# A decode step with grouped attention on one core: K transposed by VectorE as 4-byte words, V as the stationary operand, and a new order of the loads

## The chip, the cores and the metric

The kernel runs on one core of a Trainium2 chip. The time is device microseconds, from the first to the last work of one execution. Repeated executions agree within 1.5% for the kernel before. The profile is one execution, and its span is some 1.3 to 1.9 us shorter than the time. Medians are over all runs of a kernel, and slow ones are named where they matter.

Words used below. PE is the matrix engine, PEld its loading of stationary operands ("weights"), DVE is VectorE, ACT is ScalarE, SP is the engine whose queue issues the loads. A matmul contracts over the partitions (128 in the large ones here): it takes a stationary operand (here at most 128 columns) and a moving operand (some columns that stream through).

## The reference, cut to what matters

```python
# x: 1 x 512.  k_cache, v_cache: 8 heads x 16384 keys x 128, bf16.  32 query heads, 4 per K/V head.
q = layernorm(x) @ wq                      # wq 512 x 4096
scores = q . k * 128**-0.5                 # per head 4 x 16384
o = softmax(scores) @ v
h = x + o @ wo                             # wo 4096 x 512
y = layernorm(h)
# [cut] one token: the shifted groups of the mixer are all zeros, so w1 and w2 drop out
h2 = h + y + gelu(layernorm(y) @ w3) @ w4  # w3 512 x 1792, w4 1792 x 512
```

79.17 MB have to be read: 33.6 MB of K, 33.6 MB of V, 4.2 MB each of wq and wo, 3.7 MB of w3 and w4. The arithmetic is small.

One caution. With these inputs the scores are tiny and attention is nearly a plain mean, so the comparison with the reference on the chip cannot see a wrong order of keys.

## The kernel before

K arrives with keys on the partitions. For the scores it is needed with the 128 dimensions on the partitions, so PE transposes 128x128 blocks into PSUM, DVE copies eight of them at a time to SBUF, and PE uses the copies as stationary operands. In the value matmuls the probabilities are stationary (4 columns) and V moves (128 columns).

```python
# PE: transposes and scores of one block of 4096 keys
t = eng.transpose(T_ps[bb][:, u, :], knv[:, j, :], ident[:, :])
...                                                      # [cut: waits; the scores trail by one group of 8]
eng.matmul(s_ps[B % 2][:, j*REP:(j+1)*REP], kts[pb][:, u, :], QT_sb[:, REP*g:REP*g+REP])
# DVE
eng.tensor_copy(kts[bt % 2][:, :, :], T_ps[bt % 2][:, :, :])
# PE: values
eng.matmul(og[g % 2][0:REP, 0:128], ptile[:, j, :], vb[i][:, j, :], ...)
# SP: the loads, block by block (4 blocks of 1 MB per head, 8 buffers for K, 8 for V)
issue_K(B); issue_V(B)          # in the last head: all K, then all V
wq_piece(g + 1); wo_piece(g)    # 512 KB each, in rows of 1 KB
if B == 16: w3 ...              # the MLP weights in the middle of the stream
if B == 20: w4 ...
# closing of a head (FINALIZE): denominators, division, a small transpose, 16 matmuls with wo
```

The softmax here doesn't subtract the row's maximum and nothing guards it: scores larger than these inputs give would overflow.

Of the kernel before, what the change touches and what calls it, by code (L numbers as in the profile page):

```python
# [12 lines left out]
D = 512  # L13
HQ = 32
HKV = 8
SK = 16384
DH = 128
REP = HQ // HKV
# [4 lines left out]
TB = 4096  # L23
NJ = TB // 128
NBG = SK // TB
NBT = HKV * NBG
NKV = 8
OGW = 136
SCALE = 1.0 / math.sqrt(DH)
EPS = 1e-5  # L30
GELU_C = 0.044715
GELU_S = math.sqrt(2.0 / math.pi)

KMODE = ['p'] * NBT
NBATCH = 8
assert NJ % NBATCH == 0


def bass_sequential_preLN__gqa_block_cached__mixer_s_mlp__decode_kernel(
# [14 lines left out]
    with ctx:  # L54
        sb = lambda name, shape, dt: ctx.enter_context(nc.sbuf_tensor(name, shape, dt))
        ps = lambda name, shape, dt: ctx.enter_context(nc.psum_tensor(name, shape, dt))
        semaphore = lambda name: ctx.enter_context(nc.semaphore(name))

        xrow = sb("xrow", [128, D], BF16)
        row_sb = sb("row_sb", [128, D], BF16)  # L60
        ones_b = sb("ones_b", [128, 8], BF16)
        xs_f = sb("xs_f", [128, NCH], FP32)
        ln1 = sb("ln1", [128, 2 * NCH], FP32)
        ln2 = sb("ln2", [128, 2 * NCH], FP32)
        ln3 = sb("ln3", [128, 2 * NCH], FP32)
        st = sb("st", [128, 16], FP32)
        sti = sb("sti", [128, 4], mybir.dt.int32)
        c15 = sb("c15", [128, 1], FP32)
        xn_bf = sb("xn_bf", [128, NCH], BF16)
        xc_bf = sb("xc_bf", [128, NCH], BF16)  # L70
        attn = sb("attn", [128, 2 * NCH], FP32)
        xsum = sb("xsum", [128, NCH], FP32)
        final_bf = sb("final_bf", [128, NCH], BF16)
        ones_f = sb("ones_f", [128, 128], FP32)
        ident = sb("ident", [128, 128], BF16)
        act_scr = sb("act_scr", [128, 2], FP32)
        QT_sb = sb("QT_sb", [128, HQ], BF16)
        OT_sb = sb("OT_sb", [128, HQ], BF16)
        og_sb = [sb(f"og_sb{i}", [128, DH], BF16) for i in range(2)]
        rden = sb("rden", [128, 2], FP32)  # L80
        p_sb = [sb(f"p_sb{i}", [128, 4 * NJ], BF16) for i in range(2)]
        accden = [sb(f"accden{i}", [128, 16], FP32) for i in range(2)]
        rsb = [sb(f"rsb{i}", [128, REP], FP32) for i in range(2)]
        kts = [sb(f"kts{i}", [128, NBATCH, 128], BF16) for i in range(2)]
        gtmp = sb("gtmp", [128, 3 * NHC], FP32)
        hf = sb("hf", [128, NHC], FP32)
        hcol = sb("hcol", [128, NHC], BF16)
        wq_sb = sb("wq_sb", [128, NCH, 2 * REP * DH], BF16)
        wo_sb = sb("wo_sb", [128, 2 * REP, D], BF16)
        w3_sb = sb("w3_sb", [128, NCH, FM], BF16)  # L90
        w4_sb = sb("w4_sb", [128, NHC, D], BF16)
        kb = [sb(f"kb{i}", [128, TB], BF16) for i in range(NKV)]
        vb = [sb(f"vb{i}", [128, NJ, 128], BF16) for i in range(NKV)]

        s_ps = [ps(f"s_ps{i}", [128, 4 * NJ], FP32) for i in range(2)]
        og = [ps(f"og{i}", [128, OGW], FP32) for i in range(2)]
        misc_ps = ps("misc_ps", [128, 96], BF16)
        OT_ps = misc_ps[:, 0:8]
        ln_ps = misc_ps[:, 16:32].bitcast(FP32)
        e_ps = misc_ps[:, 32:96].bitcast(FP32)  # L100
        T_ps = [ps(f"T_ps{i}", [128, NBATCH, 128], BF16) for i in range(2)]
        row_ps = ps("row_ps", [128, D], FP32)

        sem_x = semaphore("sem_x")
        sem_xps = semaphore("sem_xps")
        sem_rowps = semaphore("sem_rowps")
        sem_rowsb = semaphore("sem_rowsb")
        sem_wq = [semaphore(f"sem_wq{i}") for i in range(HKV)]
        sem_wo = [semaphore(f"sem_wo{i}") for i in range(HKV)]
        sem_w34 = semaphore("sem_w34")  # L110
        sem_out = semaphore("sem_out")
        sem_kt = [semaphore(f"sem_kt{i}") for i in range(NKV)]
        sem_vb = [semaphore(f"sem_vb{i}") for i in range(NKV)]
        sem_pool = semaphore("sem_pool")
        sem_identz = semaphore("sem_identz")
        sem_onesf = semaphore("sem_onesf")
        sem_qps = semaphore("sem_qps")
        sem_s = semaphore("sem_s")
        sem_v = semaphore("sem_v")
        sem_t = semaphore("sem_t")  # L120
        sem_den = semaphore("sem_den")
        sem_otps = semaphore("sem_otps")
        sem_attnps = semaphore("sem_attnps")
        sem_lnmm = semaphore("sem_lnmm")
        sem_hid = semaphore("sem_hid")
        sem_o2 = semaphore("sem_o2")
        sem_dve = semaphore("sem_dve")
        sem_c = semaphore("sem_c")
        sem_lnin = semaphore("sem_lnin")
        sem_xn = semaphore("sem_xn")  # L130
        sem_qT = semaphore("sem_qT")
        sem_rsum = semaphore("sem_rsum")
        sem_ognorm = semaphore("sem_ognorm")
        sem_otsb = semaphore("sem_otsb")
        sem_attnc = semaphore("sem_attnc")
        sem_xc = semaphore("sem_xc")
        sem_glu = semaphore("sem_glu")
        sem_hcol = semaphore("sem_hcol")
        sem_final = semaphore("sem_final")
        sem_p = semaphore("sem_p")  # L140
        sem_gexp = semaphore("sem_gexp")
        sem_ve = semaphore("sem_ve")
        sem_rstd = semaphore("sem_rstd")
        sem_acta = semaphore("sem_acta")
# [3 lines left out]
        wq_in = A_wq.rearrange("(k p) c -> p k c", p=128)  # L148
        wo_in = A_wo.rearrange("(h d) c -> d h c", d=128)
        w3_in = B_w3.rearrange("(k p) c -> p k c", p=128)  # L150
        w4_in = B_w4.rearrange("(m d) c -> d m c", d=128)

        def k_block_rows(B):
            g, blk = divmod(B, NBG)
            return A_k_cache[0, g, blk * TB:(blk + 1) * TB, :]

        def v_block_in(B):
            g, blk = divmod(B, NBG)
            return A_v_cache[0, g, blk * TB:(blk + 1) * TB, :].rearrange("(p j) d -> p j d", p=128)

        @block.sync
        def _(eng):
            def wq_piece(g):
                if g >= 2:
                    eng.wait_ge(sem_qps, g - 1)
                slot = g % 2
                eng.dma_start(wq_sb[:, :, slot * 512:(slot + 1) * 512], wq_in[:, :, g * 512:(g + 1) * 512]
                              ).then_inc(sem_wq[g], 16)

            def wo_piece(g):  # L170
                if g >= 2:
                    eng.wait_ge(sem_attnps, g - 1)
                slot = g % 2
                eng.dma_start(wo_sb[:, REP * slot:REP * (slot + 1), :],
                              wo_in[:, REP * g:REP * (g + 1), :]).then_inc(sem_wo[g], 16)

            eng.dma_start(xrow[0:1, :], A_x[0, 0:1, :]).then_inc(sem_x, 16)

            def issue_K(B):
                i = B % NKV  # L180
                if B >= NKV:
                    eng.wait_ge(sem_s, B - NKV + 1)
                if KMODE[B] == 'x':
                    eng.dma_start(kb[i][:, :], k_block_rows(B), transpose=True).then_inc(sem_kt[i], 16)
                else:
                    eng.dma_start(kb[i][:, :].rearrange("p (j d) -> p j d", d=128),
                                  k_block_rows(B).rearrange("(p j) d -> p j d", p=128)
                                  ).then_inc(sem_kt[i], 16)

            def issue_V(B):  # L190
                i = B % NKV
                if B >= NKV:
                    eng.wait_ge(sem_v, B - NKV + 1)
                eng.dma_start(vb[i][:, :, :], v_block_in(B)).then_inc(sem_vb[i], 16)

            LAST_G0 = NBT - NBG
            for B in range(NBT):
                i = B % NKV
                g, blk = divmod(B, NBG)
                if B < LAST_G0:  # L200
                    issue_K(B)
                    if B == 0:
                        eng.dma_start(wq_sb[:, :, 0:512], wq_in[:, :, 0:512]).then_inc(sem_wq[0], 16)
                    issue_V(B)
                elif B == LAST_G0:
                    for BB in range(LAST_G0, NBT):
                        issue_K(BB)
                    for BB in range(LAST_G0, NBT):
                        issue_V(BB)
                if blk == 1 and g + 1 < HKV:  # L210
                    wq_piece(g + 1)
                if blk == 2:
                    wo_piece(g)
                if B == 16:
                    eng.dma_start(w3_sb[:, :, :], w3_in).then_inc(sem_w34, 16)
                if B == 20:
                    eng.dma_start(w4_sb[:, :, :], w4_in).then_inc(sem_w34, 16)
            eng.wait_ge(sem_rowsb, 1)
            eng.dma_start(out[0, 0:1, :], row_sb[0:1, :]).then_inc(sem_out, 16)
            eng.wait_ge(sem_out, 16)  # L220
# [16 lines left out]
        def _(eng):  # L237
# [10 lines left out]
            def qT_group(g):  # L248
                if g == 0:
                    eng.wait_ge(sem_xn, 1)  # L250
# [407 lines left out]
```

## Time and profile before

| | before |
|---|---|
| time, median of the runs beside the changed kernel | 229.29 us |
| profiled span | 228.9 us |
| last load of weights, K or V complete | 201.3 us |
| from there to the end | 27.6 us |
| PE busy / DVE busy | 82% / 45% |

The page's table in 40 slices of 5.7 us. The digits are busy tenths; PEclk is the granted clock of PE in tenths; DMA is the mean busy share of the 16 DMA engines, and GB/s is what they moved.

```profile
PE   1696999799979997999879962799997999798733
PEclk9997999999967999799999997559997999769955
DMA  5999999999999999999999999999999999600000
GB/s 202 419 408 393 422 417 401 395 419 411 398 403 409 422 395 411 406 418 410 401 403 411 392 383 395 403 412 421 403 400 406 421 417 409 261 15 3 0 3 0
```

DMA stands at 9 (90% or more) through slice 34 at about 400 GB/s: the stream never pauses. After it come one slice at 6 and five in which DMA is nearly idle and PE works on, part of the time at half clock (granted 0.52 from 200 to 205 us, 0.50 from 220 us on). Shares of busy time hide this. PE's 82% looks like the bound, yet up to 195 us PE never holds up the loads: the DMA share is 1.00 or more in every stretch of 5 us from 10 to 195 us.

The costliest groups (line, engine, operation, tiles and shapes, count | busy us, mean ns of one | idle time before, and what ended it):

```profile
L538 DVE COPY kts<-T_ps 128x1024 bf16<-128x1024 bf16 x128 | 86.2, 692 | 95.5 <-PE T_ps L295 95.5
L295 PE MATMUL T_ps<-ident,kb 128*128 128x128 bf16 x1024 | 87.1, 235 | 9.3 <-issue 9.1
L325 PE MATMUL og<-vb,p_sb 128*4 128x128 bf16 x1024 | 67.9, 230 | 0.1
```

These are the transposes, their copies and the value matmuls: the work that the change removes or reshapes.

The end in stretches of 5 us (busy time and count by engine, then granted clock, DMA share, GB/s):

```profile
core 0: us, PE busy (x) PEld busy (x) DVE busy (x) ACT busy (x) POOL busy (x), PEclk, DMA share, GB/s
190.00:195.00 5.00, 4.73 (x96) 4.24 (x94) 2.50 (x5) 0.82 (x8) 0.00 (x0) 1.00 1.01 412
195.00:200.00 5.00, 3.56 (x70) 3.12 (x68) 2.69 (x9) 0.00 (x0) 0.00 (x0) 0.79 0.65 250
200.00:205.00 5.00, 5.00 (x80) 5.00 (x78) 3.21 (x5) 0.82 (x8) 0.00 (x0) 0.52 0.09 28
205.00:210.00 5.00, 4.25 (x89) 3.97 (x86) 2.03 (x3) 0.35 (x4) 0.00 (x0) 1.00 0.01 3
```

The tail in order of time (start, duration, engine, line, operation):

```profile
207.37 0.35 PE L266 MATMUL s_ps<-QT_sb,kts 128*128 128x4 bf16 x8 [0.61 <-DVE kts L538]
207.66 7.31 PE L325 MATMUL og<-vb,p_sb 128*4 128x128 bf16 x128
...
227.40 0.26 SPq L219 DMA_DIRECT2D out_dram<-row_sb  x1
```

The last scores of head 7 end at 207.7 us, 6.4 us after the last load. Then 128 value matmuls take 7.3 us (57 ns each), then come wo, the layer norm, the MLP and the output, one after the other, to 228.9 us. Almost nothing of this overlaps with a load.

### The profile page before, as it was taken

How to read it: one execution, taken by the hardware profiler on the slowest of the kernel's cores; microseconds unless marked ns; L12 is line 12 of the kernel's file. 1: busy time of each engine (PE TensorE's matmuls, PEld its weight loads, DVE VectorE, ACT ScalarE, POOL GpSimd, SP SyncE). 2: the span in 40 equal slices, each digit the busy share in tenths (PEclk: the TensorE clock that was granted, in tenths of full speed). 3: DMA queues.
4: the chain of work that ended last, by engine and by line, in shares of the span. 5: the costliest groups of instructions: out<-in, count | busy, mean ns of one | idle time of the engine just before them, and what ended most of it. 6: DMA issues, size and time to landing. Idle time of an engine off the chain costs nothing.

```text
span 228.9 us, 7736 instructions
## 1 busy us (share of the span) xinstructions
PE 186.8 (82%) x3477; PEld 169.7 (74%) x3477; DVE 103.4 (45%) x226; ACT 28.3 (12%) x260; POOL 0.7 (0%) x7
## 2 busy tenths in 40 slices
PE   1696999799979997999879962799997999798733
PEld 1585888688869885988768852698887888698633
DVE  4371555355534445245435530525551445561263
ACT  2011111012101111111101200111110112101000
POOL 1000000000000000000000000000000000000000
PEclk9997999999967999799999997559997999769955
DMA  5999999999999999999999999999999999600000
GB/s 202 419 408 393 422 417 401 395 419 411 398 403 409 422 395 411 406 418 410 401 403 411 392 383 395 403 412 421 403 400 406 421 417 409 261 15 3 0 3 0
DMA packets 20036, 79.66 MB, mean 348 GB/s; under 512 B 1314, under 2 KB 11300, under 8 KB 11812
## 3 DMA queue, kind: packets, MB, share of 16 engines
q1 hardware_dynamic: 20004, 79.17, 87.0%
q8 instruction: 27, 0.44, 0.8%
q14 instruction: 5, 0.04, 0.0%
HBM read 79.17 MB, written 0.00 MB: 346 GB/s over the span
## 4 chain that ended last, share of the span: by engine, by line
PE 65%; DVE 22%; issue 9%; DMA 3%; SPq 0%; ACT 0%; DVEq 0%
PE og L325 29%; PE T_ps L295 21%; DVE kts L538 17%; PE s_ps L266 9%; DMA wq_sb<-in_A_wq_dram 3%; PE misc_ps L346 2%; PE misc_ps L259 1%; DVE og_sb L554 1%; PE misc_ps L336 1%; PE og L332 1%; DVE OT_sb L560 1%; DVE rden L552 1%; DVE rsb L546 1%; PE misc_ps L386 0%; DVE row_sb L627 0%
## 5 line engine op out<-in xcount | busy, mean ns | idle before, releaser
L538 DVE COPY kts<-T_ps 128x1024 bf16<-128x1024 bf16 x128 | 86.2, 692 | 95.5 <-PE T_ps L295 95.5
L295 PE MATMUL T_ps<-ident,kb 128*128 128x128 bf16 x1024 | 87.1, 235 | 9.3 <-issue 9.1
L295 PEld LDWEIGHTS T_ps<-ident,kb 128*128 128x128 bf16 x1024 | 65.6, 105 | 13.2 <-issue 10.4
L325 PE MATMUL og<-vb,p_sb 128*4 128x128 bf16 x1024 | 67.9, 230 | 0.1
L325 PEld LDWEIGHTS og<-vb,p_sb 128*4 128x4 bf16 x1024 | 62.2, 92 | 0.7 <-issue 0.2
L266 PE MATMUL s_ps<-QT_sb,kts 128*128 128x4 bf16 x1024 | 45.5, 166 | 7.9 <-DVE kts L538 0.6
L266 PEld LDWEIGHTS s_ps<-QT_sb,kts 128*128 128x128 bf16 x1024 | 37.4, 98 | 17.6 <-DVE kts L538 17.4
L440 ACT ACTIVATE p_sb<-s_ps 128x32 bf16<-128x32 f32 x128 | 23.5, 198 | 183.7 <-PE s_ps L266 173.9
L440 ACT ACTIVATION_READ_ACCUMULATOR p_sb<-s_ps 128x1 f32 x128 | 23.4, 207 | 0.0
L259 PE MATMUL misc_ps<-xn_bf,wq_sb 128*128 128x1 bf16 x128 | 4.3, 163 | 3.9 <-DMA wq_sb<-in_A_wq_dram 3.9
L259 PEld LDWEIGHTS misc_ps<-xn_bf,wq_sb 128*128 128x128 bf16 x128 | 3.8, 97 | 3.9 <-issue 3.9
L346 PE MATMUL misc_ps<-OT_sb,wo_sb 128*128 128x1 bf16 x128 | 4.5, 165 | 2.0 <-DVE OT_sb L560 2.0
L336 PE MATMUL misc_ps<-ident,og_sb 4*128 4x4 bf16 x8 | 1.4, 175 | 5.4 <-DVE og_sb L554 5.4
L346 PEld LDWEIGHTS misc_ps<-OT_sb,wo_sb 128*128 128x128 bf16 x128 | 3.8, 99 | 2.7 <-DVE OT_sb L560 2.7
L336 PEld LDWEIGHTS misc_ps<-ident,og_sb 4*128 4x128 bf16 x8 | 0.7, 93 | 6.2 <-DVE og_sb L554 6.2
L332 PE MATMUL og<-ones_f,rsb 128*4 128x1 f32 x16 | 1.5, 165 | 2.9 <-DVE rsb L546 2.9
L546 DVE TENSOR_REDUCE rsb<-accden 128x4 f32<-128x16 f32 x8 | 1.3, 160 | 5.0 <-ACT p_sb L440 5.0
L552 DVE RECIPROCAL rden<-og 4x1 f32<-4x1 f32 x8 | 1.2, 156 | 5.0 <-PE og L332 5.0
L332 PEld LDWEIGHTS og<-ones_f,rsb 128*4 128x4 f32 x16 | 0.8, 84 | 3.5 <-DVE rsb L546 3.5
L568 DVE TENSOR_TENSOR attn<-attn,misc_ps 128x4 f32<-128x4 f32 x7 | 1.1, 158 | 4.6 <-PE misc_ps L346 4.6
L386 PE MATMUL misc_ps<-xc_bf,w_sb 128*128 128x1 bf16 x28 | 0.9, 166 | 2.6 <-DVE xc_bf L507 2.6
L554 DVE TENSOR_SCALAR og_sb<-og,rden 4x128 bf16<-4x128 f32 x8 | 2.7, 338 | 0.3
(71 smaller groups left out, 24.7 us busy)
## 6 DMA issues: line engine op xcount, KB each, us to landing
kb<-in_A_k_cache_dram SPq DMA_DIRECT2D x32, 1024.0 KB, 19.0
vb<-in_A_v_cache_dram SPq DMA_DIRECT2D x32, 1024.0 KB, 19.4
wq_sb<-in_A_wq_dram SPq DMA_DIRECT2D x8, 512.0 KB, 20.5
wo_sb<-in_A_wo_dram SPq DMA_DIRECT2D x8, 512.0 KB, 18.5
w_sb<-in_B_w_dram SPq DMA_DIRECT2D x2, 1792.0 KB, 21.7
xrow<-in_A_x_dram SPq DMA_DIRECT2D x1, 1.0 KB
out_dram<-row_sb SPq DMA_DIRECT2D x1, 1.0 KB
```

Of the source, the lines that this page charges most:

```text
L259: mm = eng.matmul(e_ps[:, h:h + 1], wq_sb[:, k, 512 * slot + jj * DH:512 * slot + (jj + 1) * DH], xn_bf[:, k:k + 1], start=(k == 0), stop= ...
L266: m = eng.matmul(s_ps[B % 2][:, j * REP:(j + 1) * REP], lhsT, QT_sb[:, REP * g:REP * g + REP], start=True, stop=True)
L295: t = eng.transpose(T_ps[bb][:, u, :], knv[:, j, :], ident[:, :])
L325: m = eng.matmul(og[g % 2][0:REP, 0:128], ptile[:, j, :], vb[i][:, j, :], start=(blk == 0 and j == 0), stop=(blk == NBG - 1 and j == NJ - 1))
L332: eng.matmul(og[g % 2][0:REP, 128:129], rsb[g % 2][:, 0:REP], ones_f[:, 0:1], start=True, stop=True).then_inc(sem_den, 1)
L336: eng.transpose(OT_ps[:, 0:REP], og_sb[g % 2][0:REP, 0:DH], ident[0:REP, 0:REP]).then_inc(sem_otps, 1)
L346: m = eng.matmul(e_ps[:, k:k + 1], wo_sb[:, REP * slot + jj, 128 * k:128 * (k + 1)], OT_sb[:, h:h + 1], start=(jj == 0), stop=(jj == REP - 1))
L440: a = eng.activation(p_sb[B % 2][:, i * NJ:(i + 1) * NJ], sview[:, i, :], ACTF.Exp, scale=float(SCALE), accum_out=accden[g % 2][:, i * NBG ...
L538: eng.tensor_copy(kts[bt % 2][:, :, :], T_ps[bt % 2][:, :, :]).then_inc(sem_c, 1)
L546: dop(eng.tensor_reduce(rsb[gb][:, 0:REP], accden[gb][:, 0:REP * NBG].rearrange("p (i b) -> p i b", b=NBG), AX.X, ALU.add), sem_rsum, g + 1)
L552: dop(eng.reciprocal(rden[0:REP, gb:gb + 1], og[gb][0:REP, 128:129]))
L554: dop(eng.tensor_scalar(og_sb[gb][0:REP, 0:DH], og[gb][0:REP, 0:DH], rden[0:REP, gb:gb + 1], None, ALU.mult), sem_ognorm, g + 1)
```

## The change

Its intent: take the transposing of K away from PE and PSUM, shorten the value matmuls, make the rows of the loads longer, and let the MLP weights, which are needed last, land last, so that the end of attention hides behind them.

- K is loaded in halves of a head, 2 MB, 16 KB per partition. DVE transposes blocks of 32x32 words of 4 bytes (two bf16 dimensions in one word), 4096 words per partition and instruction. The program counts on each quadrant of 32 partitions being transposed by itself, so the query becomes block-diagonal (64 columns per head, 16 per matmul) and keeps the four quadrants apart.
- In the value matmuls V is stationary (128x128) and the probabilities move (4 columns). The output comes out with the dimensions on the partitions, so the small transpose per head goes.
- K of head g+1 is loaded and scored before V of head g. The weights wq come in one load of 4 MB, whose space V uses later. w3 and w4 come last. The layer norms use ScalarE's square root, and the MLP its GELU.

```diff
-                            t = eng.transpose(T_ps[bb][:, u, :], knv[:, j, :], ident[:, :])
...
-            eng.tensor_copy(kts[bt % 2][:, :, :], T_ps[bt % 2][:, :, :]).then_inc(sem_c, 1)
+            src = bass.AP(kraw[n % NKR][:, :].bitcast(FP32).tensor, 0,
+                          [[HALF // 2, 128], [HALF // 4, 2], [32, 2 * NJ], [1, 32]])
+            dst = bass.AP(kt[g % 2][:, :].bitcast(FP32).tensor, 2 * hf,
+                          [[HALF, 128], [1, 2], [128, 2 * NJ], [4, 32]])   # a step of 4 words
+            k_free[n] = P.op("dve", lambda e: e.transpose(dst, src), k_land[n], t_qk.get(g - 2))
...
+                    lhs = bass.AP(kt[g % 2], o, [[2 * HALF, 128], [2, 128]])   # scores: every other element
...
-                    m = eng.matmul(og[g % 2][0:REP, 0:128], ptile[:, j, :], vb[i][:, j, :], ...)
+                        ot_ps[g % 2][:, 0:REP], vslot[n % NVS][:, J * DH:(J + 1) * DH],
+                        pv[:, J * NQ + a, :], ...
...
+            wo_land[g] = P.dma("sp", wo_sb[g % 2][:, :, :], wo_in[:, REP * g:REP * (g + 1), :],
+                               wo_free.get(g - 2))          # freed by the projection of head g-2
+        for g in range(G):                                  # the order on every engine
+            if g + 1 < G:
+                for hf in range(2):
+                    load_k(g + 1, hf)
+                    t_kt[g + 1] = transpose_half(g + 1, hf)
...
+            load_wo(g)
+            for a in range(NQ):
+                load_v(g, a)
+                if a == 0:
...
+                    if g + 1 < G:
+                        scores(g + 1)
+                        softmax_exp(g + 1)
+                    denominators(g)
+                    if g >= 1:
+                        project(g - 1)
+            values(g)
+        t_w3 = P.dma("sp", w3_sb[:, :, :], w3_in)
+        t_w4 = P.dma("sp", w4_sb[:, :, :], w4_in)
```

## The prediction

> **What bounds the kernel now.** Two things in series. (1) DMA: in the stretch table every 5 us window from 10 to 195 us has a DMA share of at least 1.00 at 367 to 421 GB/s. The change reads the same 79.17 MB. (2) A tail after the loads: the rate drops after 196 us and is about 0 from 201 us, but the span is 228.9 us. The PE finishes the last head's transposes and scores until 207.7, then 128 value matmuls (7.3 us), then projection, layer norm, MLP and output (14 us). So about 28 us of tail.
>
> **What the change removes.** 1024 PE transposes (87 us PE) and 128 PSUM copies (86 us DVE). Value matmuls turn from 128 moving columns (57 ns each in the 128-matmul run) to 4 columns with a 128x128 weight load; the trace has such pairs at 32 ns (28 w3 matmuls in 0.90 us).
>
> **What it adds.** 16 DVE transposes of 4096 words per partition. A DVE rate[...] can be read from the 512-element cast of the output row (0.68 us, against 0.16 us for tiny ops): estimate 4.3 us each, 8.6 us per head.[...] Scores stay 128 matmuls per head but load weights with a stride of two elements: estimate 4 to 6 us per head.
>
> **DMA.** Per-packet times of before: 1 KB packets 334 GB/s, 8 KB 411 (16 engines); a fit gives about 417 for 16 KB, 420 for 32 KB. The query weights (1 KB pieces, now long rows) and K gain: about 195 us of streaming instead of 198. The last landing is near 197 to 198 us.
>
> **Schedule.** Per head 21.7 us of DMA against 8.6 us DVE and about 10 us PE: DMA-bound in the steady state. With MLP weights last (3.7 MB, 10 us), the last V lands about 10 us before the end, and its values, projection, norm and first MLP half hide behind those loads. After the last landing remain 56 matmuls (2.3 us), one add, the output DMA (about 2 us): 5 us instead of 28.
>
> One wait should cost: the load of the last output-weight piece waits on the projection of head 5, which stands on PE behind the scores of head 7, hence behind the last K's transpose; the last V pieces queue behind it. With 4.3 us transposes and 30 ns scores it just fits; at 60 ns it stalls DMA 3 us; at 8.7 us transposes 7 us.
>
> **Predicted:** span about 205.5, time 206.5 us (before: median 1.3 us over its span); range 201 to 217. Faster by over 2%: 0.94; within 2%: 0.03; slower: 0.03.
>
> **What would show it.** DMA share near 1.0 until 197 to 200 us; no PE transposes; DVE transposes at 4.3 us each; DVE about 35% and PE below 50% busy; the MLP's second half waiting on the w4 load; a DMA gap before the last V loads of 0 to 5 us.
>
> **What would make it wrong.** The strided 16-byte-step write of the transpose at half rate or worse (at 13 us each DVE is the bound and the kernel slower than before); strided weight loads far above 60 ns; larger packets not reaching 411 GB/s; waits on the single issuing queue leaving DMA dry.

The 4.3 us per transpose are an estimate from the trace of the kernel before: (0.68 - 0.16) us / 512 is 1.0 ns per element, times 4096 words, plus 0.16 us. Some figures name no trace and are estimates too: 4 to 6 us of scores per head, 2.3 us for 56 matmuls, about 2 us for the output, the stalls of 3 and 7 us, and the 13 us at which DVE would be the bound. The nearest figures in that trace are 28 matmuls in 0.90 us and an output issued at 227.40 us, 1.5 us before the end.

## The result, and the profile after

The changed kernel takes 209.86 us (209.72 to 210.0, 4 runs) against 229.29 us for the kernel before (227.74 to 231.08, 4 runs). The ratio is 0.914 (95% interval 0.908 to 0.920). Ratios are the mean time of one kernel's fast runs over that of the other's in the same rounds, so not quite the ratio of the medians quoted. The outputs are right.

| | before | after |
|---|---|---|
| time, median | 229.29 us | 209.86 us |
| profiled span | 228.9 us | 208.1 us |
| last load of weights, K or V complete | 201.3 us | 202.2 us |
| from there to the end | 27.6 us | 5.9 us |
| PE busy / DVE busy | 82% / 45% | 36% / 59% |

The first thing to see: the loads end no earlier than before. The whole gain lies behind them (27.6 - 5.9 = 21.7 us), and 0.9 us of it was given back, for a span that is 20.8 us shorter.

The slices of the changed kernel (5.2 us each):

```profile
PE   0105115038204730373027500960086107913532
DVE  2194799963995299519970799069915992100300
DMA  6999999999999999999999999999999992699950
GB/s 243 463 403 419 431 422 392 417 431 431 383 416 439 422 389 420 431 422 394 414 436 425 393 415 438 416 404 409 425 441 379 408 402 83 231 411 432 371 175 3
```

DMA drops to 2 and 6 in slices 34 and 35, and the rate to 83 and 231 GB/s. That is a hole in the load stream of a kernel that is bound by its loads. The groups:

```profile
L226 DVE STREAM_TRANSPOSE kt<-kraw 128x4096 f32<-128x4096 f32 x16 | 117.6, 7407 | 40.0 <-DMA kraw<-in_A_k_cache_dram 40.0
L252 PE MATMUL s_ps<-Qbd,kt 128*128 128x16 bf16 x1024 | 28.6, 174 | 87.6 <-DVE OT L287 68.4
L276 PE MATMUL ot_ps<-p_sb,wq_sb 128*128 128x4 bf16 x640 | 19.0, 168 | 10.8 <-issue 5.9
```

One transpose takes 7.4 us, where 4.3 us had been predicted. The scores take 28 ns each (28.6 us / 1024) with weights at a stride of two elements, and the value matmuls, with contiguous weights, 30 ns (19.0 us / 640).

The end in stretches (columns as before):

```profile
165.00:170.00 5.00, 0.00 (x0) 0.00 (x0) 5.00 (x3) 0.00 (x0) 0.00 (x0) 1.00 1.02 421
170.00:175.00 5.00, 1.97 (x73) 1.97 (x74) 2.98 (x2) 0.00 (x0) 0.00 (x0) 1.00 0.51 210
175.00:180.00 5.00, 5.00 (x176) 5.00 (x174) 0.18 (x1) 2.63 (x10) 0.00 (x0) 1.00 0.26 72
180.00:185.00 5.00, 2.94 (x87) 2.77 (x84) 0.35 (x2) 0.00 (x0) 0.00 (x0) 1.00 1.05 411
...
195.00:200.00 5.00, 2.23 (x58) 2.08 (x58) 1.59 (x9) 2.23 (x6) 0.00 (x0) 1.00 1.06 346
200.00:205.00 5.00, 2.00 (x56) 1.94 (x56) 0.16 (x1) 0.00 (x0) 0.00 (x0) 1.00 0.09 27
```

Between 170 and 180 us the DMA share is 0.51 and 0.26. In stretches of 1 us the missing shares from 171 to 180 us add up to 6.2 us. Who waits? First SP's own waits (engine, line, what it waited for: total us, times, longest), then the timeline:

```profile
SPq L58 <- PE h_ps L296: 76.2, 6, 16.7
```

```profile
165.64 7.34 DVE L226 STREAM_TRANSPOSE kt<-kraw 128x4096 f32<-128x4096 f32 x1
...
173.03 3.58 PE L252 MATMUL s_ps<-Qbd,kt 128*128 128x16 bf16 x128 [9.23 <-DVE OT L287]
...
176.90 0.67 PE L296 MATMUL h_ps<-OT,wo_sb 128*128 128x1 bf16 x16
...
177.59 0.38 SPq L58 DMA_DIRECT2D wo_sb<-in_A_wo_dram  x1
178.01 0.98 SPq L58 DMA_DIRECT2D wq_sb<-in_A_v_cache_dram  x2
```

The second half of K of head 7 is transposed until 173.0 us. Only then can PE run the scores of head 7 (3.6 us), and behind them in its order stands the projection of head 5 (176.9 us, the h_ps line). That projection frees a buffer of wo. SP has been waiting for it to issue the load of wo for head 7 (177.59 us), and the V loads of head 7 stand behind it in the same queue. So a late transpose becomes a late matmul, a late buffer, a late issue, and then an idle stream.

The very end:

```profile
192.76 1.02 PE L276 MATMUL ot_ps<-p_sb,vown 128*128 128x4 bf16 x32 [1.48 <-DMA vown<-in_A_v_cache_dram]
...
202.37 2.00 PE L376 MATMUL ot_ps<-hcol,w_sb 128*128 128x1 bf16 x56 [3.50 <-DMA w_sb<-in_B_w_dram]
204.41 0.16 DVE L381 TENSOR_TENSOR fin<-xsum,ot_ps 128x4 bf16<-128x4 f32 x1 [6.74 <-PE ot_ps L376]
204.59 0.35 SPq L58 DMA_DIRECT2D out_dram<-fin  x1
```

The last V values run at 192.8 us. Everything from there to the first half of the MLP is hidden behind the loads of w3 and w4. After the last load 56 matmuls (2.0 us), an addition and the output remain.

### The profile page after: what moved, and what is told of

The parts are those of the page before. It is cut to its first block, busy times and chain, and to the rows that moved or that the text cites. A ratio compares the mean times of both kernels' runs of the same rounds, so it can differ in the third digit from the quotient of the medians.

```text
span 208.1 us, 5140 instructions
## 1 busy us (share of the span) xinstructions
PE 74.0 (36%) x2441; PEld 72.0 (35%) x2441; DVE 123.4 (59%) x64; ACT 16.1 (8%) x77; POOL 0.5 (0%) x5
## 4 chain that ended last, share of the span: by engine, by line
DMA 43%; DVE 25%; PE 15%; issue 14%; SPq 1%; ACT 0%
DMA kraw<-in_A_k_cache_dram 29%; DVE kt L226 23%; DMA w_sb<-in_B_w_dram 10%; PE s_ps L252 7%; DMA xcol<-in_A_x_dram 4%; PE ot_ps L276 3%; PE ot_ps L215 2%; SPq L58 1%; PE ot_ps L376 1%; PE den_ps L266 1%; PE h_ps L296 1%; DVE Qbd L238 0%; PE den_ps L193 0%; DVE OT L287 0%; PE ot_ps L234 0%
## 5 line engine op out<-in xcount | busy, mean ns | idle before, releaser
L226 DVE STREAM_TRANSPOSE kt<-kraw 128x4096 f32<-128x4096 f32 x16 | 117.6, 7407 | 40.0 <-DMA kraw<-in_A_k_cache_dram 40.0
L252 PE MATMUL s_ps<-Qbd,kt 128*128 128x16 bf16 x1024 | 28.6, 174 | 87.6 <-DVE OT L287 68.4
L252 PEld LDWEIGHTS s_ps<-Qbd,kt 128*128 128x128 bf16 x1024 | 27.9, 104 | 88.2 <-DVE OT L287 68.9
L276 PE MATMUL ot_ps<-p_sb,wq_sb 128*128 128x4 bf16 x640 | 19.0, 168 | 10.8 <-issue 5.9
L276 PEld LDWEIGHTS ot_ps<-p_sb,wq_sb 128*128 128x128 bf16 x640 | 18.1, 103 | 11.3 <-issue 6.3
L260 ACT ACTIVATE p_sb<-s_ps 128x128 bf16<-128x128 f32 x32 | 8.4, 277 | 157.0 <-PE s_ps L252 157.0
L276 PE MATMUL ot_ps<-p_sb,vown 128*128 128x4 bf16 x384 | 11.6, 168 | 6.6 <-issue 3.7
L276 PEld LDWEIGHTS ot_ps<-p_sb,vown 128*128 128x128 bf16 x384 | 11.1, 104 | 6.9 <-issue 3.8
L296 PEld LDWEIGHTS h_ps<-OT,wo_sb 128*128 128x128 bf16 x128 | 6.0, 125 | 2.5 <-issue 2.1
L260 ACT ACTIVATION_READ_ACCUMULATOR p_sb<-s_ps 128x1 f32 x32 | 6.6, 207 | 0.0
```

What stands on the lines that cost most here:

```text
L226: k_free[n] = P.op("dve", lambda e: e.transpose(dst, src), k_land[n], t_qk.get(g - 2))
L252: t = P.op("pe", lambda e, J=J, l=lhs, r=rhs, be=be: e.matmul(s_ps[g % 2][:, 16 * J:16 * J + 16], l, r, start=(be == 0), stop=(be == 3)), ...
L260: t_exp[g] = P.op("act", lambda e, h=h: e.activation(p_sb[g % 2][:, h * 128:(h + 1) * 128], src[:, h, :], ACTF.Exp, scale=float(SCALE), ac ...
L276: t = P.op("pe", lambda e, J=J, a=a, n=n: e.matmul(ot_ps[g % 2][:, 0:REP], vslot[n % NVS][:, J * DH:(J + 1) * DH], pv[:, J * NQ + a, :], s ...
L296: t = P.op("pe", lambda e, h=h, k=k, l=lhs: e.matmul(h_ps[:, k:k + 1], l, OT[g % 2][:, h:h + 1], start=False, stop=(g == G - 1 and h == RE ...
```

## The experiments

Twelve runs, in the order of the argument. Each was timed beside the kernel before on the same chip, except e1 (one look).

### 1. Why a transpose takes 7.4 us

The destination is written with a step of four words, 16 bytes. In e1 heads 2 and 3 write with a step of one word and heads 4 and 5 with a step of two. The scores of these heads are wrong on purpose.

```diff
+            step = 1 if g in (2, 3) else 2 if g in (4, 5) else 4
+            o_hf, s_hi = {1: (64, 32), 2: (64, 1), 4: (2, 1)}[step]
-            dst = ... 2 * hf,      [[HALF, 128], [1, 2],    [128, 2 * NJ], [4, 32]]
+            dst = ... o_hf * hf,   [[HALF, 128], [s_hi, 2], [128, 2 * NJ], [step, 32]]
```

> Wrong result on purpose. The transposes of heads 2 and 3 write with a step of one word, those of heads 4 and 5 with a step of two words, all others with a step of four words (16 bytes) as in the changed kernel, where they took 7.33 to 7.62 us. Theory A (the write step costs the extra time): step 1 takes about 4.3 us, step 2 between 4.3 and 6 us, step 4 stays at 7.4. Theory B[...]: all 7.4 us. Theory C (traffic of the loads or of the weight reads slows it): all near 7.4, with the shortest ones where the loads are idle. The time of the kernel hardly moves, since head 7 is unchanged.

Theory B is that a transpose of 4-byte words takes this long whatever the step.

DVE's timeline, one line each for a transpose of head 1 (step 4), head 2 (step 1), head 4 (step 2) and head 6 (step 4):

```profile
37.50 7.36 DVE L228 STREAM_TRANSPOSE kt<-kraw 128x4096 f32<-128x4096 f32 x1
...
50.28 4.45 DVE L228 STREAM_TRANSPOSE kt<-kraw 128x4096 f32<-128x4096 f32 x1 [5.42 <-DMA kraw<-in_A_k_cache_dram]
...
92.95 4.45 DVE L228 STREAM_TRANSPOSE kt<-kraw 128x4096 f32<-128x4096 f32 x1 [11.85 <-DMA kraw<-in_A_k_cache_dram]
...
137.04 7.38 DVE L228 STREAM_TRANSPOSE kt<-kraw 128x4096 f32<-128x4096 f32 x1 [11.89 <-DMA kraw<-in_A_k_cache_dram]
```

All eight transposes with a step of one or two words took 4.45 us, and all eight with a step of four took 7.3 to 7.6 us, under the same load traffic. So the write step is the cause. An inherent cost of 4-byte transposes and contention with the loads are ruled out. At a step of one or two words the estimate of the prediction (4.3 us) nearly holds: 4096 words in 4.45 us are 1.09 ns per word. Only these three steps were measured, and why a step of four costs more than one of two is not shown. The time of the kernel stayed (209.93 us, one run), as expected with head 7 left as it was.

### 2. Is the hole the wait for the wo buffer?

e2 adds a third buffer for wo and changes nothing else. Head 7 then waits for the projection of head 4, which is long done.

```diff
-        wo_sb = [... for i in range(2)]      # and g % 2, wo_free.get(g - 2)
+        wo_sb = [... for i in range(3)]      # and g % 3, wo_free.get(g - 3)
```

> One more buffer for the output weights, so that the load for head 7 no longer waits for the projection of head 5 behind the scores of head 7. Theory (the 6 us gap in the loads at 172 to 179 us comes from this wait, and the loads are the bound): the gap shrinks to under 1.5 us and the time falls by 4.5 to 6.5 us, to about 204 us. Rival (the gap comes from the V slots, which are freed by the value matmuls of head 6 at the same moment): the gap keeps over 3 us, and the time falls by under 2 us.

204.39 us (204.34 to 204.91), ratio to before 0.889 (0.886 to 0.893). The stretches of e2 (same columns as above):

```profile
170.00:175.00 5.00, 1.86 (x69) 1.86 (x70) 3.08 (x2) 0.00 (x0) 0.00 (x0) 1.00 1.03 406
175.00:180.00 5.00, 5.00 (x176) 5.00 (x173) 0.18 (x1) 2.63 (x10) 0.00 (x0) 1.00 0.86 325
```

The hole is gone but for 0.7 us at 175 to 180 us. The last load completes at 196.9 in place of 202.2 us, 5.3 us earlier, and the time falls by 5.5 us. The rest is the rival of the expectation: at 178.6 us SP issues V loads that had waited for a V slot. The transposes are still at 7.4 us here, so what cost was the chain from the last of them to a load. In e1 eight of them were 3 us shorter and the time did not move. Both say that their slowness costs little by itself.

### 3. Do faster transposes help? (failed, for another reason)

To write contiguously and keep the result right, K's rows must be dealt to the partitions differently. e6 does that with four loads of 32 partitions in place of one load of 128.

```diff
-            k_land[n] = P.dma("sp", kraw[n % NKR][:, :], src, ...)
+            src = A_k_cache[0, g].rearrange("(a c p j) d -> a p c (j d)", a=4, c=4, p=32)
+            k_land[n] = [P.dma("sp", kraw[n % NKR][32 * a:32 * a + 32, :]..., src[a, ...], ...) for a in range(4)]
-                          [[HALF, 128], [1, 2], [128, 2 * NJ], [4, 32]])
+                          [[HALF, 128], [32, 2], [128, 2 * NJ], [1, 32]])
```

> The changed kernel with the transposes writing contiguously (K is loaded with its rows dealt to the partitions so that the result stays right: four loads of 32 partitions instead of one of 128). Nothing else changed. Theory (the write step makes the transpose late, and the lateness of head 7 makes the gap in the loads): transposes 4.45 us, those of head 7 end about 5 us earlier, the gap shrinks from 6.2 us to 1 to 2.5 us, time 204.5 to 206.5 us. Rival (the gap does not follow from the transpose): transposes 4.45 us and time within 1 us of 209.9.

291.3 to 291.5 us in its three fast runs (a slow one took 297.1), ratio 1.272: both theories missed it. From e6's page, slices of 7.2 us and the transposes:

```profile
DMA  7999999999999999999999999999999999989990
GB/s 165 274 430 220 208 214 209 322 401 207 213 211 421 283 214 206 337 382 209 215 242 418 265 220 205 345 362 212 217 218 420 265 215 212 338 334 396 432 322 8
L227 DVE STREAM_TRANSPOSE kt<-kraw 128x4096 f32<-128x4096 f32 x16 | 71.1, 4446 | 164.2 <-DMA kraw<-in_A_k_cache_dram 164.2
```

The transposes took 4.45 us as expected, but while K is loaded the rate is 205 to 220 GB/s, half of what it was, although the DMA engines count as busy. e10 was the same idea with a step of two words and rows of 16 KB, together with the other ideas of this section:

> Combination: transposes with a write step of two words (K dealt so that each partition reads one 16 KB run), three buffers of output weights, x issued first on the queue of the loads, and w4 loaded in long rows and in two halves. Theory: no gap in the loads, w4 at over 400 GB/s; loads end near 194 us, the second MLP half needs 1 us after the last of them, time 199.5 to 202.5 us. If w4 in long rows brings nothing, 202 to 204.

It took 287.8 and 288.4 us in its two fast runs, ratio 1.258; four more runs were slow, up to 312.0 us. Its 16 KB packets show the loss per packet: the median was 1247 ns, against 614 ns for packets of the same size in the changed kernel. In rate that is 215 against 422 GB/s over 16 engines (from the means).

Is it the number of loads or the 32 partitions? e13 also makes four loads of each half, but cuts along the row, so that each covers all 128 partitions.

```diff
+            k_land[n] = [P.dma("sp", kraw[n % NKR][:, c * HALF // 4:(c + 1) * HALF // 4],
+                               src[:, c * HALF // 4:(c + 1) * HALF // 4], ...) for c in range(4)]
```

> Control for the slow K loads of 32 partitions each: the changed kernel with each half of K loaded in four loads too, but cut along the row, each over all 128 partitions (4 KB per partition). Theory[...]: K packets of 4 KB at 390 to 410 GB/s, time 209 to 213 us. Rival (four loads in place of one, with their 64 issues and completions, cost the time): over 240 us.

What the theory comes to is that the loads were slow because each covered 32 partitions, not because there were four of them.

212.96 us (ratio 0.931). Its 4 KB packets moved at 400 GB/s, and K took 84.0 us of streaming in place of 79.5 (the packets' time, divided by 16), which is enough for the 3.1 us that the kernel lost. So four loads in place of one cost little (3.1 us), and the loads into 32 partitions ran at half the rate (215 against 422 GB/s). Why they do is not shown. The other way tried, leaving K as it is and reordering the columns as the weights are loaded, did not build, so there is no run of it. Whether faster transposes would gain anything was therefore not tried at full load rate. Section 2 makes it unlikely.

### 4. What the order of the loads is worth

e3 moves the MLP weights of the changed kernel from the end into heads 4 and 5:

```diff
+            if g == 4: t_w3 = P.dma("sp", w3_sb[:, :, :], w3_in)
+            if g == 5: t_w4 = P.dma("sp", w4_sb[:, :, :], w4_in)
```

> The MLP weights are loaded after the V of heads 4 and 5, not last. Theory (loading them last hides about 6 us of the tail): the V of head 7 lands last, and after it follow 1 us of values, projection, norm 3.4 us, both MLP halves 4.5 us and the output 3 us, so 12 us instead of 6, time 215 to 217 us. Rival (the tail is hidden anyway, or the earlier MLP load takes up the gap before the last V): time within 1 us of the changed kernel.

215.15 us (214.96 to 215.34), ratio 0.936. In its profile the last V completes at 202.0 us and the end is at 213.4: 11.3 us of tail in place of 5.9. Loading the MLP weights last is worth 5.3 us here. e3 also shows a part of the gain that no run tested alone: from the end of its last value matmul to the end of the program it takes 10.2 us, where the kernel before took 13.9, so the rewritten closing (division, projection, layer norm, MLP, output) is itself 3.7 us shorter. Part of that may be the clock, which was 0.50 in the last 9 us of the kernel before and 1.0 in e3. The same one step on the kernel before is e5:

```diff
-                if B == 16: w3 ...
-                if B == 20: w4 ...
+                if B == NBT - 1: w3 ... ; w4 ...
```

> The kernel before, with only the load order of the MLP weights changed: last, behind V of head 7. Theory (the tail of before is the matrix engine's work after the last K has landed): the last K lands 9 us earlier, and as the matrix engine keeps up with the loads the time falls by 6 to 9 us, to about 222 us. Rival (the matrix engine, 82% busy, is itself behind at that point): under 3 us.

223.97 us against 230.14, ratio 0.974 (0.968 to 0.979). A change of two lines in the old kernel gives about 6 us.

e9 takes back the loading of K one head ahead, in the order of the loads and of PE:

```diff
+            load_wo(g); load_v(g, 0..3); denominators(g); values(g)
+            if g + 1 < G:
+                load_k(g + 1, hf); transpose_half(g + 1, hf)   # both halves
+                normalize(g); scores(g + 1); softmax_exp(g + 1); project(g)
```

> The changed kernel without loading K one head ahead: loads in the order K, output weights, V of the same head, and the matrix engine in the order scores, values of the same head. Theory A (the look-ahead pays only to hide the latency of the last head, and costs the gap): loads never pause, they end near 195 us; values of head 7 are ready about 3 us after the last load, time 205 to 208 us, a little faster than 209.9. Theory B (the look-ahead is needed to keep the loads busy): pauses in the loads at every head, time over 215 us.

206.62 us (206.13 to 206.67), ratio 0.902 (0.896 to 0.908). Its DMA line:

```profile
DMA  6999999999999999999999999999999999999800
```

The loads never pause and complete at 197.2 us (15 of the 16 engines are done at 195.8). But the values of head 7 now come so late that 7.6 us are left after the last load (204.8 - 197.2). So the look-ahead was not needed to keep the loads busy. It shortens the tail by about 1.7 us (7.6 against 5.9), and with two wo buffers it costs a hole of 6 us. With three buffers (e2) only the good half remains.

### 5. What V as the stationary operand is worth alone

e8 puts this one part into the kernel before:

```diff
-                    m = eng.matmul(og[g % 2][0:REP, 0:128], ptile[:, j, :], vb[i][:, j, :], ...)
+                    m = eng.matmul(og[g % 2][:, 0:REP], vb[i][:, j, :], ptile[:, j, :], ...)
```

> The kernel before with one part of the change alone: V is the stationary operand of the value matmuls (4 moving columns in place of 128), and the output comes out transposed, so the small transpose of each head goes too. Theory (only the 128 value matmuls and the closing of head 7 in the tail count): values 7.3 us become 3.6 us, closing 1 us shorter, time 225 to 226.5 us. Rival (matrix-engine time counts in the load-bound stretch as well, 34 us are saved in all): under 220 us.

221.75 us against 229.51, ratio 0.968 (0.962 to 0.974): between the two expectations. The tail of e8 on PE:

```profile
201.06 0.35 PE L266 MATMUL s_ps<-QT_sb,kts 128*128 128x4 bf16 x8 [0.34 <-DVE kts L534]
201.27 3.77 PE L325 MATMUL og<-p_sb,vb 128*128 128x4 bf16 x128
```

The 128 values take 3.8 in place of 7.3 us, as expected. But the last scores also end 6.3 us earlier (201.4 against 207.7 us), although the loads are no earlier (the last K lands at 190.0 against 189.9 us, the last load at 202.7 against 201.3 us). In the kernel before PE was some 6 us behind the loads when they ended, and nearly 30 ns saved on each value matmul (57 to 29 ns) let it catch up in part: in e8 PE waits for a load of K four times (2.5 us in all, the last at 130 us), in the kernel before it never does. A higher clock is not the reason, since the mean granted clock was lower in e8 (0.72 against 0.90), and the transposes took 277 ns in the mean against 235, so part of the saving seems to be lost again there. The theory had counted only the work after the last load and forgotten this backlog. So matrix-engine time in a load-bound stretch was not free here, because the engine had a backlog at its end.

### 6. The start

In the changed kernel x is issued from ScalarE's queue beside the big loads and lands at 8.3 us, 7.6 us after its issue. e4 issues it first on SP, where it lands 1.7 us after its issue (queue and order changed together).

```diff
-        t_x = P.dma("act", xcol[:, :], ...)
+        t_x = P.dma("sp", xcol[:, :], ...)
```

> Only x's load moved from ScalarE's queue to the front of the queue of the loads. In the changed kernel it landed at 8.3 us. Theory (the start is hidden, the loads bind from 5 us on): x lands near 2 to 3 us, the first transpose starts 3 to 5 us earlier, and the time stays within 1 us of 209.9. Rival (the late x delays the whole chain): 3 us or more faster.

```profile
2.50 0.17 DVE L190 CAST ln<-xcol 128x4 f32<-128x4 bf16 x1
...
8.71 7.38 DVE L226 STREAM_TRANSPOSE kt<-kraw 128x4096 f32<-128x4096 f32 x1 [3.88 <-DMA kraw<-in_A_k_cache_dram]
...
18.55 3.55 PE L215 MATMUL ot_ps<-xn,wq_sb 128*128 128x1 bf16 x128 [15.03 <-DMA wq_sb<-in_A_wq_dram]
```

The layer norm starts at 2.5 in place of 8.3 us and the first transpose at 8.7 in place of 10.6, but the query projection still waits for wq, until 18.5 us. The time is 210.27 us (210.0 to 210.44): the same. What was late at the start, while the loads ran, cost nothing here.

### 7. A combination

e12 keeps K's loads, with three wo buffers, the last two V pieces in a free K buffer, x first, and w4 in long rows and two halves. Long rows of w4 mean that the columns of w3 are loaded as weights with a step of 14 elements.

> Combination that leaves K loaded as in the changed kernel (transposes stay at 7.4 us): three buffers of output weights; the last two V pieces of head 7 go into a K buffer that is free by then; x issued first on the queue of the loads; w4 in long rows and two halves. Theory: no gap over 0.5 us in the loads from 10 us on, w4 at over 400 GB/s, 1 us of matmuls after the last load; time 200.5 to 203 us, at least 1.5 us under the run with three buffers alone (204.4). If slower than 204, one of these parts costs.

204.41 us (204.25 to 204.58), ratio 0.894 (0.889 to 0.898): not better than e2. The packets took 1.6 us less than in e2 (194.1 against 195.7 us, divided by 16), but the last load completed at nearly the same time (196.8 against 196.9 us; the "2 us earlier" in the next expectation is not what the landings show). And PE no longer waits for it at the end. The end had moved to the chain from the last V, and on it:

```profile
193.85 3.52 PE L375 MATMUL s_ps<-xc,w_sb 128*128 128x1 bf16 x56 [1.36 <-DVE st L362]
```

The 56 matmuls of the first MLP half took 3.5 us, against 1.65 with contiguous columns. e14 takes 2 KB rows of w4 (a step of 2) and loads the last wo behind the last V.

```diff
-        w4_in = B_w4.rearrange("(m d) c -> d m c", d=128)
+        w4_in = B_w4.rearrange("(m d r) c -> d m r c", d=128, r=2)
+        load_wo(G - 1)        # behind values(G - 1), and w4 in two loads
```

> The combined kernel mended. Its run showed the loads ending 2 us earlier, but the first MLP half took 3.5 us in place of 1.6 (weights loaded with a step of 14 elements) and the chain from the last V, which landed at 189.1 us, had become the last to end. Now w4 is loaded in 2 KB rows (weights of w3 loaded with a step of 2, as in the scores, where it cost nothing), in two parts, and the last output weights are loaded behind the last V. Theory: first MLP half 1.7 us, last V about 1 us earlier, time 201 to 203 us. Rival (the step is not what cost, or the tail cannot be shortened further): 204 us or more.

203.34 us (203.11 to 203.9), ratio 0.886 (0.882 to 0.890), a little above the expected range. The first MLP half:

```profile
193.90 1.65 PE L378 MATMUL s_ps<-xc,w_sb 128*128 128x1 bf16 x56 [1.36 <-DVE st L365]
```

So the step was what had cost. A pair of weight load and matmul took 29 ns at a step of 1 (1.65 us / 56 in e2) and of 2 (1.65 us / 56 here; the scores 28), 36 ns at 4 (2.00 us / 56, the second MLP half of e2) and 63 ns at 14 (3.52 us / 56 in e12). What e14 gains on e2 (1.0 us) comes after the last load, which completes no earlier (197.0 against 196.9 us): with w4 in two loads only 24 matmuls are left then, where e2 has 56 (2.0 us).

```profile
197.17 0.93 PE L388 MATMUL ot_ps<-hcol,w_sb 128*128 128x1 bf16 x24 [0.51 <-DMA w_sb<-in_B_w_dram]
```

The last V lands at 185.2 us, 2.4 us earlier than in e2, but PE pauses in the midst of a run of value matmuls, where it waits for nothing that the profile shows:

```profile
185.47 0.65 PE L285 MATMUL ot_ps<-p_sb,kraw 128*128 128x4 bf16 x19
189.18 0.99 PE L285 MATMUL ot_ps<-p_sb,kraw 128*128 128x4 bf16 x31 [3.06 <-issue]
```

The profile books these 3.1 us as "issue". Pauses at the same place, after 19 value matmuls of their run, appear in e2 (2.2 us) and e12 (2.8 us) too. What PE waits for there is not shown. In e14 the pause does not set the end: PE still waits 0.5 us for the last load (the line above). In the changed kernel PE waits for V near that place (1.48 us before the matmuls at 190.27 and again before those at 192.76 us), and its trace shows no such pause there. e14 is the fastest version tried: 6.5 us (3.1%) under the changed kernel by the medians, in separate rounds.

## Why the prediction was right or wrong

The time (206.5 predicted, 201 to 217 the range, 209.86 measured) and its main reason were right. The terms:

- **"Two things in series", the loads and "about 28 us of tail": right.** Tail 27.6 us. e5 and e8 shortened it from two sides with the loads left as long, and gained 6 and 8 us.
- **"5 us instead of 28" after the last landing: right.** Measured 5.9 us; w4 was the last wait, as said. e3 shows how much the order did: 11.3 us without it.
- **"About 195 us of streaming instead of 198": right.** The packets' time in the trace, divided by 16, sums to 195.3 us (before: 201.2).
- **"The last landing is near 197 to 198 us": wrong, 202.2 us.** This is the step that failed, and it is why the span was 208.1 and not 205.5 us. The prediction had counted no pause of the loads ("it just fits"), and the hole of 6.2 us took back the 5.9 us that the faster streaming saved. Of the 3.4 us by which the time was missed, the other 0.8 us is that it exceeds the span by 1.9 and not by 1.0 us.
- **"4.3 us each" for the transposes: wrong in size,** 7.4 us. The cause is the step of 16 bytes in the write (e1). The prediction had named this as what could make it wrong, and had priced it: "at 8.7 us transposes 7 us" of pause. Measured: 7.4 us transposes, 6.2 us of pause. That there is no pause at 4.3 us was not tested at the full load rate (section 3).
- **"The load of the last output-weight piece waits on the projection of head 5": right,** shown by e2, which takes away this wait alone and gains 5.5 us.
- **Scores "4 to 6 us per head", "at 60 ns it stalls": too careful.** 3.6 us per head, 28 ns each: the stride of two elements cost nothing here.
- **DVE "about 35%" busy: wrong, 59%,** from the transposes. It stays off the critical path but for its last use. **PE "below 50%": right,** 36%.
- Not foreseen: x landing at 8.3 us (e4: free), and that the look-ahead of K is not needed to keep the loads busy (e9).

## What to carry to other kernels

In a kernel bound by its loads, count two things only: the pauses of the load stream, and the work between the last byte and the end. Then order the loads so that the bytes that need the least work land last. For each load ask which buffer it waits for and which engine frees that buffer: with one issuing queue, a single wait on a matmul that stands far back in PE's order held up everything behind it (a hole of 6.2 us here), and the cure may be 4 KB per partition of one more buffer (5.5 us in e2). Faster work off that path gained nothing here (the transposes of e1, the start in e4), but check first that its engine is not behind when the loads end (e8). And a layout that helps an engine can cost far more in the loads, as the 32-partition loads did (291 us in e6).
